# Output projection of the last two token blocks as a seven-product 2x2 block multiplication, and small VectorE instructions given to other engines

## Chip, cores and metric

The kernel runs on one core of a Trainium2 chip. Its time is the device time of one execution in microseconds (us); the figure compared is the median over several runs. One execution of it was also recorded by the hardware profiler. The engines are TensorE (PE in the rows; PEld is its weight load), VectorE (DVE), ScalarE (ACT), GpSimd (POOL) and SyncE (SP), which here issues transfers.

## The reference, cut to what matters

```python
# q, k, v: 4 batches, 8 heads, 576 positions, 64 features
out_d = sm_attn(mean of 4 neighbours of q, k, v)          # 144 x 144 scores per head
out_local = sm_attn(q, k, v, mask=|i - j| < 4)            # a band of 7 keys
x = repeat(out_d, 4) + out_local                          # 2304 tokens x 512
# moe:  w_in 512 x 2048, w_out 2048 x 512, alpha per column
h = x @ w_in
x = (np.maximum(h, 0.0) + alpha * np.minimum(h, 0.0)) @ w_out
# moe2: w_gate, w_val 512 x 1536, w_out 1536 x 512
xn = x / np.sqrt(np.mean(x * x, axis=-1, keepdims=True) + 1e-06) * rms_g
g = xn @ w_gate
return (g * (1.0 / (1.0 + np.exp(-g))) * (xn @ w_val)) @ w_out
```

All of it is in f32.

## The kernel before

**Matmuls.** Each f32 operand is split into an upper half in f16 and a lower half, the f16 of what is left. A product is three f16 matmuls: upper by upper, upper by lower and lower by upper. The helper `split` (L430) makes the halves: ACT writes the upper one (L432), and DVE subtracts it from the scaled source (L433). `halves` (L1646) does the same without a scale, ACT at L1647 and DVE at L1648.

**Blocks and stages.** The 2304 tokens are six blocks of 384 (BW). A block m goes through `m1(m)`, the first expert (products `hps` at L1445, then ReLU parts `g` on ACT and DVE, `ghl` their halves, and the sums over 2048 in four PSUM tiles `acc` at L1462); `m1_evac` takes `acc` to `x1` on ACT (L1476), scaled by a column `inv` that DVE multiplies before it (L1474). Then comes the normalisation: squares on ACT (L1371), their sums `ra` over four pieces on DVE (L1376), a power on POOL (L1397), the factor spread by TensorE into `rps`, and in `xn` the product `ra<-x,rps` (L1419) and its split into the halves `x`. Then `m2(m)`: gate and value products `gps` (L1581), tanh on ACT, the product `th` (L1595) and the value product (L1598) on DVE, the halves `uhl`, and the output product `oacc` (L1610).

**The last two blocks.** Blocks 4 and 5 go through the second expert together in `m2_pair`. Their gate and value products are already a 2x2 block multiplication with seven products (tiles `pa`, `pb`, `pf`, L1758), over 12 groups f of 128 of the 1536 columns. The output product follows (L1819): for each block and each of three tiles of 128 tokens 12 x 3 matmuls of 512 columns, 216 in all. ACT evicts the left half of a tile (L1825) and then DVE the right one (L1826), and a transfer writes it.

**The attention beside it.** The local attention of each block is computed on DVE and POOL, while TensorE does the stages of earlier blocks: POOL multiplies (`prod`, 128x896, L538 with the keys and L592 with the values), and DVE sums (L549, L605). `sm1` and `sm2` are the softmax between them. `trans` transposes the result into the PSUM tile `xps`, DVE adds the downsampled attention into an SBUF tile `xs` (L642), and `split` makes the halves `xt` that `m1` reads.

**Order.** The program is written in groups; the last statement, `issue_order(tc, nc, groups)`, puts the instructions of every engine in a fixed order by a list schedule with costs that stand in the file, and the table `LEADS` shifts ranges of groups by hand (first group, last group, ns). Every engine then works through its own list in that order and waits by semaphores, so an instruction whose operands are late holds up all behind it on its engine.

## Time and profile before

| | |
|---|---|
| median of 3 runs | 948.97 us (948.82 to 949.27) |
| the profiled execution, its own time | 947.25 us |
| its span in the trace | 945.5 us |
| TensorE busy | 911.5 us, 96% of the span |
| VectorE busy | 668.6 us, 71% |
| ScalarE busy | 509.3 us, 54% |
| GpSimd busy | 241.0 us, 25% |

The time of an execution and the span differ by what lies before the first and after the last record. A term that is read from the trace is set against the time of the profiled execution, and that against the median.

The stages by the profile: to 110 us the weights are read and split, and the first dense attention; 110 to 240 the first block's first expert; 240 to 390 the second expert of blocks 0 and 1; 390 to 540 the first expert of blocks 2 and 3; 540 to 610 the second expert of block 2; 610 to 740 the first expert of blocks 4 and 5; 740 to 812 the second expert of block 3; 812 to 894 gate and value of the pair; 894 to 941.2 its output product; then the last eviction and transfer.

### The profile page before, as it was taken

To read this page: it belongs to the slowest core of one execution; us is meant where nothing else is said; L and a number is where in the kernel's file an instruction comes from. 1 tells how busy PE (TensorE), PEld (TensorE's weight loads), DVE (VectorE), ACT (ScalarE), POOL (GpSimd) and SP (SyncE) were. 2 spreads that over 40 slices of the span, in tenths; PEclk is the share of its full clock that TensorE was granted. 3 is DMA by queue.
4 is the path that set the end of the run, shared out by engine and by line. 5 is a ranking of instruction groups with operands and counts; after the bars stand their busy time and mean duration, and the time that the engine had idled before them with its cause. 6 is when DMAs were issued, how large, how long until landed. Compare 5 with 4: busy or idle time off the path is not lost.

```text
span 945.5 us, 16369 instructions
## 1 busy us (share of the span) xinstructions
PE 911.5 (96%) x6412; PEld 589.4 (62%) x6412; DVE 668.6 (71%) x1281; ACT 509.3 (54%) x1163; POOL 241.0 (25%) x167
## 2 busy tenths in 40 slices
PE   6968999999999999999999999999999999999998
PEld 4856878699665565555666555556666565555543
DVE  4789996788899966988876889497476246356510
ACT  5899889789972374233665322243443333456410
POOL 1101100340333405776205668251131000000000
PEclk9989999999999999999999999999999999999999
DMA  9785534446321222221141211010000000100001
GB/s 243 261 263 177 158 118 120 163 140 227 108 84 59 72 86 86 95 79 53 54 124 34 84 51 34 6 29 2 1 1 1 1 1 1 32 3 2 1 23 44
DMA packets 53711, 73.78 MB, mean 78 GB/s; under 512 B 22190, under 2 KB 35138, under 8 KB 53634
## 3 DMA queue, kind: packets, MB, share of 16 engines
q1 hardware_dynamic: 53634, 72.74, 24.9%
q8 instruction: 50, 0.82, 0.3%
q14 instruction: 27, 0.22, 0.1%
...
## 4 chain that ended last, share of the span: by engine, by line
PE 79%; DVE 9%; ACT 8%; DMA 2%; issue 2%; SPq 0%; POOL 0%; ACTq 0%; DVEq 0%; POOLq 0%
PE acc L1462 18%; PE hps L1445 17%; PE gps L1581 16%; PE oacc L1610 7%; PE oacc L1819 5%; PE pa L1758 4%; PE pf L1758 2%; DMA out_dram<-ob 1%; ACT wr L1179 1%; DVE lo L605 1%; PE pb L1758 1%; ACT wi L432 1%; ACT wr L1182 1%; ACT dls L969 1%; PE avps L766 1%
## 5 line engine op out<-in xcount | busy, mean ns | idle before, releaser
L1445 PE MATMUL hps<-xt,wi 128*128 128x192 f16 (+1 forms) x1536 | 324.3, 287 | 6.3 <-DVE g L433 2.3
L1581 PE MATMUL gps<-x,w 128*128 128x384 f16 x1152 | 244.5, 326 | 6.0 <-DVE th L1595 5.2
L1462 PE MATMUL acc<-ghl,wo 128*128 128x384 f16 (+1 forms) x960 | 235.9, 310 | 0.5 <-ACT ob L1639 0.2
L1445 PEld LDWEIGHTS <-wi 128*128 128x128 f16 x1536 | 145.6, 99 | 57.4 <-issue 5.6
L1462 PEld LDWEIGHTS <-wo 128*128 128x128 f16 x1344 | 127.9, 98 | 61.1 <-issue 2.9
L1581 PEld LDWEIGHTS <-w 128*128 128x128 f16 x1152 | 113.0, 99 | 81.0 <-issue 7.9
L1610 PE MATMUL oacc<-w,uhl 128*128 128x512 f16 x432 | 143.5, 379 | 0.0
L538 POOL TENSOR_TENSOR prod<-cq,ckv 128x896 f32<-128x896 f32 x48 | 104.4, 2193 | 130.6 <-ACT dd L735 40.5
L592 POOL TENSOR_TENSOR prod<-ls,ckv 128x896 f32<-128x896 f32 x48 | 86.0, 1867 | 103.2 <-issue 49.7
L1451 DVE SCALAR_TENSOR_TENSOR hps<-g,oma,hps 128x192 f32<-128x192 f32 (+1 forms) x128 | 66.0, 517 | 38.6 <-ACT g L1449 37.4
L1449 ACT ACTIVATE g<-hps 128x384 f32<-128x384 f32 x96 | 47.2, 492 | 82.7 <-PE hps L1445 82.5
L1610 PEld LDWEIGHTS <-uhl 128*128 128x128 f16 x432 | 42.5, 99 | 43.7 <-issue 1.9
L1462 PE MATMUL acc<-g,wo 128*128 128x192 f16 (+1 forms) x384 | 65.8, 286 | 0.0
L432 ACT ACTIVATE ghl<-hps,grp 128x384 f16<-128x384 f32 (+1 forms) x73 | 41.9, 576 | 36.2 <-DVE hps L1451 29.8
L1601 ACT ACTIVATE uhl<-gps 128x384 f16<-128x384 f32 x48 | 23.4, 488 | 58.2 <-DVE gps L1598 43.2
L433 DVE SCALAR_TENSOR_TENSOR ghl<-hps,grp,ghl 128x384 f16<-128x384 f32 (+1 forms) x73 | 44.1, 605 | 14.6 <-ACT ghl L432 14.4
L605 DVE TENSOR_REDUCE lo<-prod 128x128 f32<-128x896 f32 x48 | 51.6, 1078 | 3.6 <-POOL prod L592 3.2
L549 DVE TENSOR_REDUCE ls<-prod 128x14 f32<-128x896 f32 x48 | 51.7, 1077 | 2.4 <-POOL prod L538 2.4
L1719 POOL TENSOR_TENSOR wt<-w 128x768 f32<-128x768 f16 x16 | 26.4, 1650 | 73.4 <-DVE wi L1648 58.8
L1179 ACT ACTIVATE wr<-wr 128x768 f32<-128x768 f32 (+1 forms) x48 | 42.3, 887 | 4.9 <-DMA wr<-in_moe_w_in_dram 2.9
L1819 PE MATMUL oacc<-w,wo 128*128 128x512 f16 x180 | 42.9, 379 | 0.0
L1594 ACT ACTIVATE th<-gps,tsc 128x384 f32<-128x384 f32 x36 | 20.7, 577 | 40.2 <-PE gps L1581 40.2
...
## 6 DMA issues: line engine op xcount, KB each, us to landing
...
```

The source lines that it names most:

```text
L538: engs[i].tensor_tensor(out=pr, in0=view(st["q"][:, j, t:t + TP], [[D, TP], [0, ND], [1, D]]), in1=view(st["k"][:, j, t:t + TP], [[D, TP], ...
L549: nc.vector.tensor_reduce(out=st["s"][:, j, t:t + TP], in_=st.pop(("p", i)), axis=AX.X, op=ALU.add)
L592: engs[i].tensor_tensor(out=over(pr, i), in0=view(st["s"][:, j, t:t + TP], [[ND, TP], [1, ND], [0, D]]), in1=view(st["v"][:, j, t:t + TP], ...
L605: nc.vector.tensor_reduce(out=st["o"][:, t:t + TP, j], in_=view(pr, [[ND * D, TP], [ND, D], [1, ND]]), axis=AX.X, op=ALU.add)
L1179: nc.scalar.activation(out=hi.bitcast(F32), in_=hi.bitcast(F32), func=AF.Prelu, scale=2.0 ** -112, alpha=2.0 ** 32)
L1445: nc.tensor.matmul(ps[:, j], wi[:, f + j, a, kk * 128:(kk + 1) * 128], x[:, b_, kk, c0:c0 + n], start=(i == 0), stop=(i == 3 * KK - 1))
L1451: nc.vector.scalar_tensor_tensor(out=ps[:, j], in0=g[:, j], scalar=oma[:, f + j:f + j + 1], in1=ps[:, j], op0=ALU.mult, op1=ALU.add)
L1462: nc.tensor.matmul(acc[e], wo_f(f)[:, a, e * 128:(e + 1) * 128], hl[:, b_], start=(f == f0 and i == 0), stop=(f == f1 and i == 2))
L1581: nc.tensor.matmul(ps, w2_t[i0 + f // 3].rearrange("p a (k c) -> p a k c", k=KK)[:, a, kk, (f % 3) * 128:(f % 3 + 1) * 128], xh[:, b_, kk] ...
L1610: nc.tensor.matmul(acc[tt], t[:, a, tt * 128:(tt + 1) * 128], w[:, b_, f % 3], start=(f in first and i == 0), stop=(f in last and i == 2))
L1758: nc.tensor.matmul(ps, w[:, a, kk, c:c + 128], x[:, b_, kk], start=(start and n == 0), stop=(n == 3 * K2 - 1), skip_group_check=True)
L1819: nc.tensor.matmul(acc, uhl(f)[:, h, a, tt * 128:(tt + 1) * 128], w[:, b_, f % 3], start=(f == 0 and i == 0), stop=(f == NF2 - 1 and i == 2))
```

## The change

**The output product of the pair** becomes a 2x2 block multiplication with seven products. The blocks are: the two token blocks by two halves of the 1536 columns (6 groups g each), and the weight by its row halves and column halves (256 columns each). `outp` makes one product for one tile of 128 tokens: 6 x 3 matmuls of 256 columns; there are 7 x 3 of these, 378 matmuls, into the PSUM tiles `px` and `py`. `usums` makes the sums and differences of the left operand on POOL, two for each of the first six f and three for each of the last six, and their halves; `wsums` does it for the weights (for each g two sums that put the f32 value back together from its halves, and four differences). `scaled` writes halves with a constant factor, ACT the upper and DVE the lower one. `fma` on DVE adds a product to what was evicted before.

**Small instructions** move from DVE: the sums `ra` of the normalisation, the lower halves `x` in `xn`, and the mask, maximum and normalising steps of the local softmax to POOL; `inv`, `dsum` (12 of 16) and a constant's addition to ACT. The sum of the two attentions stays in PSUM, and `split` reads it there.

**The table of shifts** `LEADS` is new, 53 lines for 45; the first line of each stands for it below. Counted on the two programs: TensorE has 378 matmuls where it had 216 in the output product and is otherwise the same; POOL has 284 instructions for 172, ACT 1068 for 1009, DVE 1239 for 1263.

```diff
-    (5553, 5613, 20500), (6925, 6974, 3000), (8480, 8741, -2500), (3702, 3837, 500), (545, 591, -4500),
+    (8269, 8277, -4000), (3290, 3494, -500), (6599, 6626, -500), (7948, 7994, -15500), (5847, 6045, -12500),
...
-            nc.vector.tensor_tensor(out=s, in0=s, in1=m.unsqueeze(3).to_broadcast([128, 2, T, ND]), op=ALU.subtract)
+            nc.gpsimd.tensor_tensor(out=s, in0=s, in1=m.unsqueeze(3).to_broadcast([128, 2, T, ND]), op=ALU.subtract)
...
-            nc.vector.tensor_scalar(out=m, in0=m, scalar1=1e-9, scalar2=None, op0=ALU.add)
+            nc.scalar.activation(out=m, in_=m, func=AF.Copy, bias=1e-9)
             nc.vector.reciprocal(m, m)
-            nc.vector.tensor_tensor(out=s, in0=s, in1=m.unsqueeze(3).to_broadcast([128, 2, T, ND]), op=ALU.mult)
+            nc.gpsimd.tensor_tensor(out=s, in0=s, in1=m.unsqueeze(3).to_broadcast([128, 2, T, ND]), op=ALU.mult)
...
-                xs = att.tile([128, HP, TH * NC], F32, tag="xs", name="xs")
-                ps = ps.rearrange("p t (c r h) -> p t h c r", h=HP, r=2)
-                xv = xs.rearrange("p h (t c r) -> p t h c r", t=TH, r=2)
+                pv = ps.rearrange("p t (c r h) -> p t h c r", h=HP, r=2)
...
+                        pa = pv[:, a - s0:e - s0, :, :, r]
                         nc.vector.tensor_tensor(
-                            out=xv[:, a - s0:e - s0, :, :, r],
-                            in0=ps[:, a - s0:e - s0, :, :, r],
+                            out=pa, in0=pa,
                             in1=od[:, :, :, o].unsqueeze(1).to_broadcast([128, e - a, HP, NC // 2]),
                             op=ALU.add)
...
-                split(x[:, 0, :, c0:c0 + TH * NC], x[:, 1, :, c0:c0 + TH * NC], xs, col(S_X0 + b))
+                split(x[:, 0, :, c0:c0 + TH * NC], x[:, 1, :, c0:c0 + TH * NC],
+                      view(ps, [[1, HP], [HP, TH * NC]]), col(S_X0 + b))
...
-            nc.vector.tensor_scalar(out=sm, in0=sm, scalar1=1e-9, scalar2=4.0, op0=ALU.add, op1=ALU.mult)
+            nc.scalar.activation(out=sm, in_=sm, func=AF.Copy, scale=4.0, bias=4e-9)
...
-                    nc.vector.tensor_tensor(out=st["a"], in0=st["a"], in1=a, op=ALU.add)
+                    nc.gpsimd.tensor_tensor(out=st["a"], in0=st["a"], in1=a, op=ALU.add)
...
-                nc.vector.tensor_tensor(out=x, in0=x1_t[m][:, e], in1=st["r"], op=ALU.mult)
-                split(xh_t[m][:, 0, e], xh_t[m][:, 1, e], x, rgx[:, e:e + 1])
+                nc.vector.scalar_tensor_tensor(out=x, in0=x1_t[m][:, e], scalar=rgx[:, e:e + 1], in1=st["r"],
+                                               op0=ALU.mult, op1=ALU.mult)
+                nc.scalar.activation(out=xh_t[m][:, 0, e], in_=x, func=AF.Copy)
+                nc.gpsimd.tensor_tensor(out=xh_t[m][:, 1, e], in0=x, in1=xh_t[m][:, 0, e], op=ALU.subtract)
...
-            nc.vector.tensor_tensor(out=inv1[:, b:b + 1], in0=col(INV1_0 + b), in1=col(INVW), op=ALU.mult)
+            if b not in inv_done:
+                inv_done.add(b)
+                nc.scalar.activation(out=inv1[:, b:b + 1], in_=col(INV1_0 + b), func=AF.Copy, scale=col(INVW))
...
+        def scaled(o, x, c):
+            nc.scalar.activation(out=o[:, 0], in_=x, func=AF.Copy, scale=c)
+            nc.vector.scalar_tensor_tensor(out=o[:, 1], in0=x, scalar=c, in1=o[:, 0], op0=ALU.mult, op1=ALU.subtract)
+
+        def wsums(g):
+            ra = att.tile([128, DM], F32, tag="da", name="wr1")
+            rb = ob_p.tile([128, DM], F32, tag="ob", name="wr2")
+            for r, f in ((ra, g), (rb, g + F2)):
+                nc.gpsimd.tensor_tensor(out=r, in0=wof(f)[:, 0], in1=wof(f)[:, 1], op=ALU.add)
+            a1, a2, b1, b2 = ra[:, 0:ED], ra[:, ED:DM], rb[:, 0:ED], rb[:, ED:DM]
+            for o, x, y in ((a1, a2, a1), (a2, b2, a2), (b2, b2, a1), (b1, b1, b2)):
+                nc.gpsimd.tensor_tensor(out=o, in0=x, in1=y, op=ALU.subtract)
+            scaled(t13[g], ra, 0.5)
+            scaled(t2(g), b2, 1.0)
+            scaled(wof(g)[:, :, ED:DM], b1, 1.0)
...
+        def usums(f, ga, gb):
+            g = f % F2
+            G = nc.gpsimd
+            x, y = f32(A21[g]), f32(S3F[g])
+            if f < F2:
+                scaled(two(A11[g]), ga, 1.0)
+                G.tensor_tensor(out=y, in0=ga, in1=x, op=ALU.subtract)
+                scaled(two(S3[g]), y, 0.5)
+                return
+            scaled(two(A12[g]), ga, 1.0)
+            scaled(two(A22[g]), gb, 1.0)
+            G.tensor_tensor(out=x, in0=x, in1=gb, op=ALU.add)
+            G.tensor_tensor(out=y, in0=gb, in1=y, op=ALU.subtract)
+            z = prod_p.tile([128, BW], F32, tag="prod", name="s4")
+            G.tensor_tensor(out=z, in0=ga, in1=y, op=ALU.subtract)
+            scaled(two(S1[g]), x, 0.5)
+            scaled(two(S2[g]), y, 0.25)
+            scaled(two(S4[g]), z, 0.25)
...
-            value(f, ga, A, 0)
-            value(f, gb, s3_, 1)
-
-        for h, m in enumerate((ma, mb)):
-            for tt in range(NT):
-                n = h * NT + tt
-                tag = ("a0", "at", "w", "a1", "at", "a2")[n]
-                acc = pool_of(tag).tile([128, DM], F32, tag=tag, name="oacc")
-                for f in range(NF2):
-                    w = w2_t[8 + f // 3].rearrange("p a (f e) -> p a f e", f=3)
-                    for i, (a, b_) in enumerate(((0, 0), (0, 1), (1, 0))):
-                        nc.tensor.matmul(acc, uhl(f)[:, h, a, tt * 128:(tt + 1) * 128], w[:, b_, f % 3],
-                                         start=(f == 0 and i == 0), stop=(f == NF2 - 1 and i == 2))
-                TQ = 128 // NC
-                tag = "prod" if h == 0 else "raw"
-                o = pool_of(tag).tile([128, DM], F32, tag=tag, name="ob")
-                HD = DM // 2
-                nc.scalar.activation(out=o[:, 0:HD], in_=acc[:, 0:HD], func=AF.Copy, scale=col(INV2))
-                nc.vector.tensor_scalar(out=o[:, HD:DM], in0=acc[:, HD:DM], scalar1=col(INV2), scalar2=None,
-                                        op0=ALU.mult)
-                if h:
-                    b, t = divmod(m * 2 * T + tt * TQ, TT)
-                    assert t + TQ <= TT and b > 0
-                    nc.sync.dma_start(out=bass.AP(tensor=out.tensor, offset=out.offset + (b * S + t) * DM,
-                                                  ap=[[TT * DM, NC], [DM, TQ], [1, DM]]), in_=o)
-                else:
-                    rows_out(o, m, tt)
+            value(f, ga, ga, A)
+            value(f, f32(A21[f]) if f < F2 else gb, gb, s3_)
+            if f == F2 // 2:
+                places()
+            usums(f, ga, gb)
+            if F2 // 2 <= f < F2 // 2 + F2:
+                wsums(f - F2 // 2)
...
-        for h, m in enumerate((ma, mb)):
-            for tt in range(NT):
-                n = h * NT + tt
-                tag = ("a0", "at", "w", "a1", "at", "a2")[n]
-                acc = pool_of(tag).tile([128, DM], F32, tag=tag, name="oacc")
-                for f in range(NF2):
-                    w = w2_t[8 + f // 3].rearrange("p a (f e) -> p a f e", f=3)
-                    for i, (a, b_) in enumerate(((0, 0), (0, 1), (1, 0))):
-                        nc.tensor.matmul(acc, uhl(f)[:, h, a, tt * 128:(tt + 1) * 128], w[:, b_, f % 3],
-                                         start=(f == 0 and i == 0), stop=(f == NF2 - 1 and i == 2))
-                TQ = 128 // NC
...
-                nc.scalar.activation(out=o[:, 0:HD], in_=acc[:, 0:HD], func=AF.Copy, scale=col(INV2))
-                nc.vector.tensor_scalar(out=o[:, HD:DM], in0=acc[:, HD:DM], scalar1=col(INV2), scalar2=None,
-                                        op0=ALU.mult)
...
+        def outp(ps, u, w, tt, start):
+            for g in range(F2):
+                for i, (a, b_) in enumerate(((0, 0), (0, 1), (1, 0))):
+                    nc.tensor.matmul(ps, two(u[g])[:, a, tt * 128:(tt + 1) * 128], w(g, b_),
+                                     start=(start and g == 0 and i == 0), stop=(g == F2 - 1 and i == 2),
+                                     skip_group_check=True)
+
+        def fma(o, ps, c, x):
+            nc.vector.scalar_tensor_tensor(out=o, in0=ps, scalar=col(c), in1=x, op0=ALU.mult, op1=ALU.add)
+
+        oa, ob = [xt_p.tile([128, NT, DM], F32, tag="xt", name="ob") for _ in range(2)]
+        X, s1, s2 = [], [], []
+        for tt in range(NT):
+            tag = ("a0", "w", "at")[tt]
+            x = pool_of(tag).tile([128, 2, ED], F32, tag=tag, name="px")
+            X.append(x)
+            outp(x[:, 1], A12, b2(0), tt, True)
+            outp(x[:, 0], A11, b1, tt, True)
+            t = wk.tile([128, ED], F32, tag="mm", name="so")
+            nc.scalar.activation(out=t, in_=x[:, 0], func=AF.Copy, scale=col(INV2))
+            fma(oa[:, tt, 0:ED], x[:, 1], INV2, t)
+            s1.append(t)
+        for tt in range(NT):
+            outp(X[tt][:, 0], A22, lambda g, b_: wof(g)[:, b_, ED:DM], tt, False)
+            t = hl_p.tile([128, ED], F32, tag="hl", name="so")
+            nc.scalar.activation(out=t, in_=X[tt][:, 0], func=AF.Copy, scale=col(INV2))
+            s2.append(t)
+        for tt in range(NT):
+            tag = ("a1", "w", "at")[tt]
+            F_, G_ = pool_of(tag).tile([128, ED], F32, tag=tag, name="py"), X[tt][:, 1]
+            o4, o5 = oa[:, tt], ob[:, tt]
+            outp(F_, S1, s13(0), tt, True)
+            fma(o5[:, ED:DM], F_, INV8, s1[tt])
+            outp(G_, S2, lambda g, b_: t2(g)[:, b_], tt, True)
+            fma(o4[:, ED:DM], G_, INV8, s1[tt])
+            outp(F_, S4, b2(1), tt, False)
+            fma(o4[:, ED:DM], F_, INV8, o4[:, ED:DM])
+            rows_out(o4, ma, tt)
+            outp(G_, S3, s13(1), tt, False)
+            fma(o5[:, 0:ED], G_, INV8, s2[tt])
+            fma(o5[:, ED:DM], G_, INV8, o5[:, ED:DM])
```

**TensorE, the end of the gate and value products.** `pa` and `pf` are gate products, `oacc` (before) and `px` (after) the output product; behind the arrow stands first the operand that streams through TensorE and then the one that is loaded before it; the names are those of buffers, which hold several things in turn. Before:

```order
L1758 LDWEIGHTS w_4015
L1758 MATMUL pa<-xc,w_4015 128x384
L1819 LDWEIGHTS wo
L1819 MATMUL oacc<-w_3111,wo 128x512
L1758 LDWEIGHTS w_4015
L1758 MATMUL pa<-xc,w_4015 128x384
L1819 LDWEIGHTS wo
L1819 MATMUL oacc<-w_3111,wo 128x512
```

After:

```order
L1825 LDWEIGHTS w_4015
L1825 MATMUL pa<-xc,w_4015 128x384
L1908 LDWEIGHTS wi
L1908 MATMUL px<-w_3803,wi 128x256
L1825 LDWEIGHTS w_4015
L1825 MATMUL pa<-xc,w_4015 128x384
L1825 LDWEIGHTS wi
L1825 MATMUL pf<-xc,wi 128x384
```

Output matmuls stand between the last gate matmuls in both; after the change they have 256 columns.

**TensorE, the first `py` matmul,** the first whose two operands are sums made by POOL (`ts` holds those of the weight, `w_3245` here those of the left operand). After:

```order
L1908 LDWEIGHTS wo
L1908 MATMUL px<-w_3458,wo 128x256
L1908 LDWEIGHTS wi
L1908 MATMUL px<-w_3111,wi 128x256
L1908 LDWEIGHTS w_3245
L1908 MATMUL py<-ts,w_3245 128x256
L1908 LDWEIGHTS wi
L1908 MATMUL px<-w_3111,wi 128x256
```

It stands behind 87 `px` matmuls that follow the last gate product; before the change there are `oacc` matmuls here and no operand from POOL.

**GpSimd, the end of its list.** `wt` are sums for the weights of the gate products, `ry` the power of the normalisation; `wr` are sums of the output weight, `wo` and `s` sums of the left operand (`th`). Before:

```order
L1719 TENSOR_TENSOR wt<-w_3592 128x768
L1719 TENSOR_TENSOR wt<-w_4015 128x768
L1719 TENSOR_TENSOR wt<-w_3935 128x768
L1719 TENSOR_TENSOR wt<-w_4015 128x768
L1719 TENSOR_TENSOR wt<-w_3935 128x768
L1397 TENSOR_TENSOR ry<-ry,mhalf 128x3 x2
```

After:

```order
L1810 TENSOR_TENSOR wr_9912<-w_4145 128x512
L1813 TENSOR_TENSOR wr_9911<-wr_9912,wr_9911 128x256
L1856 TENSOR_TENSOR wo<-th,wo 128x384
L1813 TENSOR_TENSOR wr_9912<-wr_9912,wr_9911 128x256
L1858 TENSOR_TENSOR s_9988<-th,wo 128x384
L1856 TENSOR_TENSOR wo<-th,wo 128x384
L1813 TENSOR_TENSOR wr_9912<-wr_9912 128x256
L1858 TENSOR_TENSOR s_10059<-th,wo 128x384
L1856 TENSOR_TENSOR wo<-th,wo 128x384
L1855 TENSOR_TENSOR wo<-wo,th 128x384 x2
L1858 TENSOR_TENSOR s_10130<-th,wo 128x384
L1855 TENSOR_TENSOR wo<-wo,th 128x384
```

Before, POOL's list ended with the normalisation of the last block; after, it ends with the sums that the output product reads.

**VectorE, from block 3's first expert to block 2's second.** Before:

```order
L433 SCALAR_TENSOR_TENSOR ghl<-hps,grp,ghl 128x384
L605 TENSOR_REDUCE lo<-prod 128x2x64 x2
L1474 TENSOR_TENSOR inv_106<-sc 128x1
L605 TENSOR_REDUCE lo<-prod 128x2x64
L1474 TENSOR_TENSOR inv_106<-sc 128x1
L1376 TENSOR_TENSOR ra<-ra 128x384
L1595 SCALAR_TENSOR_TENSOR th<-th,gps 128x384
L642 TENSOR_TENSOR xs<-xps,outd 128x3x4x16
L1598 SCALAR_TENSOR_TENSOR gps<-th,kap,gps 128x384
L1376 TENSOR_TENSOR ra<-ra 128x384
L1602 TENSOR_TENSOR uhl<-gps,uhl 128x384
```

After:

```order
L442 SCALAR_TENSOR_TENSOR ghl<-hps,grp,ghl 128x384
L614 TENSOR_REDUCE lo<-prod 128x2x64
L650 TENSOR_TENSOR xps<-xps,outd 128x3x4x16
L650 TENSOR_TENSOR xps<-xps,outd 128x2x4x16
L650 TENSOR_TENSOR xps<-xps,outd 128x4x16
L614 TENSOR_REDUCE lo<-prod 128x2x64
L442 SCALAR_TENSOR_TENSOR xt<-xps,sc,xt 128x4x96
L558 TENSOR_REDUCE ls<-prod 128x14
L650 TENSOR_TENSOR xps<-xps,outd 128x4x16
L650 TENSOR_TENSOR xps<-xps,outd 128x2x4x16
L1616 SCALAR_TENSOR_TENSOR th<-th,gps 128x384
```

The two `inv` and the `ra` sums between the reductions and `th` are gone from this list; the sums of the attention now write `xps`, and the lower half `xt` reads it.

## Rows read from the trace of the kernel before

**Rows 1.** Page, the span and part 1: busy time, share and instructions of each engine.

```profile
span 945.5 us, 16369 instructions
...
PE 911.5 (96%) x6412; PEld 589.4 (62%) x6412; DVE 668.6 (71%) x1281; ACT 509.3 (54%) x1163; POOL 241.0 (25%) x167
```

**Rows 2.** Busy time by stretch: length, PE, PEld, DVE, ACT, POOL; PEclk, DMA, GB/s.

```profile
0.00:110.00 110.00, 89.07 (x853) 73.30 (x854) 87.47 (x237) 94.08 (x275) 15.79 (x43) 0.97 0.73 220
...
540.00:610.00 70.00, 66.86 (x385) 37.92 (x384) 56.33 (x88) 18.50 (x38) 41.77 (x24) 1.00 0.12 34
...
812.00:894.00 82.00, 81.69 (x497) 48.35 (x496) 44.69 (x76) 44.62 (x80) 0.00 (x0) 1.00 0.04 10
894.00:941.20 47.20, 47.20 (x221) 21.41 (x219) 7.37 (x14) 6.01 (x11) 0.00 (x0) 1.00 0.08 23
941.20:945.50 4.30, 0.03 (x1) 0.00 (x0) 0.68 (x2) 0.47 (x1) 0.00 (x0) 0.99 0.32 122
```

**Rows 3.** TensorE's timeline, 192-column matmuls: start us, duration, engine, line, operation.

```profile
145.41 2.15 PE L1445 MATMUL hps<-xt,wi 128*128 128x192 f16 x24
147.40 0.33 PE L1462 MATMUL acc<-g,wo 128*128 128x384 f16 x1
```

**Rows 4.** TensorE's timeline, 512-column matmuls of the last stage.

```profile
926.17 11.82 PE L1819 MATMUL oacc<-w,wo 128*128 128x512 f16 x54
937.83 0.38 PE L1819 MATMUL oacc<-w,uhl 128*128 128x512 f16 x1
```

**Rows 5.** TensorE's waits, 110 us on: total us, times, longest us.

```profile
PE gps L1581 <- DVE th L1595: 5.2, 6, 1.3
PE hps L1445 <- DVE ghl L433: 1.3, 2, 0.9
PE qkps L713 <- DVE xs L642: 0.5, 1, 0.5
```

**Rows 6.** TensorE's timeline around 543 us, idle time before it in brackets.

```profile
542.88 2.27 PE L1581 MATMUL gps<-x,w 128*128 128x384 f16 x13 [1.33 <-DVE th L1595]
```

**Rows 7.** VectorE's timeline, two long instructions.

```profile
540.13 1.76 DVE L1474 TENSOR_TENSOR inv<-sc 128x1 f32<-128x1 f32 x1 [0.43 <-ACT x L1476]
...
577.24 2.25 DVE L433 SCALAR_TENSOR_TENSOR x<-ra,rgx,x 128x384 f16<-128x384 f32 x1
```

**Rows 8.** GpSimd's timeline, the products beside them.

```profile
539.78 2.09 POOL L538 TENSOR_TENSOR prod<-cq,ckv 128x896 f32<-128x896 f32 x1 [1.09 <-DVE lo L605]
...
576.99 2.08 POOL L538 TENSOR_TENSOR prod<-cq,ckv 128x896 f32<-128x896 f32 x1 [1.24 <-issue]
```

**Rows 9.** VectorE's groups by form: count, busy us, mean ns, idle before.

```profile
L433 DVE SCALAR_TENSOR_TENSOR ghl<-hps,grp,ghl 128x384 f16<-128x384 f32 x71 | 43.3, 611 | 14.5 <-ACT ghl L432 14.4
...
L433 DVE SCALAR_TENSOR_TENSOR xt<-xs,sc,xt 128x384 f16<-128x384 f32 x16 | 17.7, 1109 | 0.1
L1648 DVE TENSOR_TENSOR wo<-th,wo 128x384 f16<-128x384 f32 x20 | 15.6, 786 | 7.3 <-ACT wo L1647 6.9
L433 DVE SCALAR_TENSOR_TENSOR x<-ra,rgx,x 128x384 f16<-128x384 f32 x16 | 14.9, 944 | 0.0
...
L1376 DVE TENSOR_TENSOR ra<-ra 128x384 f32<-128x384 f32 x15 | 8.5, 564 | 2.7 <-ACT ra L1371 2.7
L1474 DVE TENSOR_TENSOR inv<-sc 128x1 f32<-128x1 f32 x9 | 8.4, 939 | 5.8 <-ACT x L1476 5.8
```

**Rows 10.** GpSimd's groups by form.

```profile
L1719 POOL TENSOR_TENSOR wt<-w 128x768 f32<-128x768 f16 x16 | 26.4, 1650 | 73.4 <-DVE wi L1648 58.8 <-DVE wsr L1648 10.3 <-DVE wt L1724 4.0
L979 POOL TENSOR_TENSOR dls<-dls,dlsum 96x408 f32<-96x408 f32 x12 | 11.2, 955 | 106.7 <-DVE eb L425 60.6 <-DVE sc L1261 25.8 <-ACT g L1449 9.2
...
L1397 POOL TENSOR_TENSOR ry<-ry,mhalf 128x3 f32<-128x3 f32 x6 | 5.2, 873 | 76.5 <-DVE ry L1396 75.5 <-DVE eb L425 0.9
```

**Rows 11.** ScalarE's timeline, the last eviction.

```profile
941.27 0.47 ACT L1825 ACTIVATE ob<-oacc,sc 128x256 f32<-128x256 f32 x1 [0.39 <-PE oacc L1819]
```

**Rows 12.** VectorE's timeline, the last eviction.

```profile
941.77 0.48 DVE L1826 TENSOR_SCALAR ob<-oacc,sc 128x256 f32<-128x256 f32 x1 [0.38 <-ACT ob L1825]
```

More of the change, by code (lines that the diff above doesn't have):

```diff
@@ L398 @@
     INV1_0 = S_X0 + B
+    INV8 = INV1_0 + B
     def eb(i):
@@ L1466, in m1_acc @@
         return [ps_a.tile([128, n], F32, tag=f"a{e}", name=f"acc{e}") for e in range(KK)]
+    inv_done = set()
     def m1_evac(m, acc, c0, n):
@@ L1739, in m2_pair @@
             scr += [w2_t[4 + i][:, a, 0:PW].bitcast(F32) for a in range(2)]
-        last = {}
-        def uhl(f):
-            if f < 10:
-                t = wo[:, f * 2 * BW:(f + 1) * 2 * BW]
-            else:
-                if not last:
-                    last["t"] = raw_p.tile([128, 4 * BW], F32, tag="raw", name="uhl")
-                t = last["t"][:, (f - 10) * 2 * BW:(f - 9) * 2 * BW]
-            return t.bitcast(F16).rearrange("p (h a n) -> p h a n", h=2, a=2)
+        F2, ED = NF2 // 2, DM // 2
@@ new lines, in m2_pair, with part @@
+        wif = wi.rearrange("p f a c -> p (f a c)")
+        w2f = {i: w2_t[i].rearrange("p a w -> p (a w)") for i in range(3)}
+        def part(t, n):
+            return t[:, n * 2 * BW:(n + 1) * 2 * BW]
+        wos = [wo[:, n * BW:(n + 1) * BW].bitcast(F16) for n in range(21)]
+        spare = []
+        freed = [[part(w2f[1], n) for n in range(4)] + [part(wif, n) for n in range(8)] +
+                 [w2_t[4 + i][:, a, PW:2 * PW] for i in (0, 1) for a in range(2)],
+                 [part(w2f[2], n) for n in range(4)] + [part(wif, 8 + n) for n in range(8)] +
+                 [w2_t[6][:, a, PW:2 * PW] for a in range(2)]]
@@ new lines, in m2_pair, with places @@
+        A11, A21, S3F, S3 = wos[0:F2], wos[F2:2 * F2], wos[2 * F2:3 * F2], wos[3 * F2:]
+        A12, A22, S1, S2, S4 = [], [], [], [], []
+        t13, t4 = [], []
+        def places():
+            r = raw_p.tile([128, 4 * BW], F32, tag="raw", name="us").bitcast(F16)
+            S3.extend(part(r, n) for n in range(3))
+            freed[1].append(part(r, 3))
+            for l in freed:
+                for g in range(3):
+                    for x, n in zip((A12, A22, S1, S2, S4), range(5)):
+                        x.append(l[5 * g + n])
+            for _ in range(2):
+                t = raw_p.tile([128, 4 * BW], F32, tag="raw", name="ts").bitcast(F16)
+                t13.extend(t[:, g * 2 * DM:(g + 1) * 2 * DM].rearrange("p (a e) -> p a e", a=2) for g in range(3))
@@ new lines, in two, with f32, wof, t2 @@
+        def two(x):
+            return x.rearrange("p (a n) -> p a n", a=2)
+        def f32(x):
+            return x.bitcast(F32)
+        def wof(f):
+            return w2_t[8 + f // 3].rearrange("p a (f e) -> p a f e", f=3)[:, :, f % 3]
+        def t2(g):
+            return w2f[0][:, g * DM:(g + 1) * DM].rearrange("p (a e) -> p a e", a=2)
+        def scaled(o, x, c):
+            nc.scalar.activation(out=o[:, 0], in_=x, func=AF.Copy, scale=c)
+            nc.vector.scalar_tensor_tensor(out=o[:, 1], in0=x, scalar=c, in1=o[:, 0], op0=ALU.mult, op1=ALU.subtract)
@@ L1771, in gate, with value @@
             return th
[L1773 to L1774 removed]
+        def value(f, o, u, v):
+            nc.vector.scalar_tensor_tensor(out=o, in0=u, scalar=kps[:, f // 3:f // 3 + 1], in1=v, op0=ALU.mult,
                                            op1=ALU.mult)
[L1776 to L1781 removed]
+        def usums(f, ga, gb):
[16 more added lines that the diff above has]
+            scaled(two(S4[g]), z, 0.25)
         xa, xb = xh_t[ma], xh_t[mb]
@@ new lines, in m2_pair @@
+        for tt in range(NT):
[17 more added lines that the diff above has]
+            fma(o5[:, ED:DM], G_, INV8, o5[:, ED:DM])
+            TQ = 128 // NC
+            b, t = divmod(mb * 2 * T + tt * TQ, TT)
+            assert t + TQ <= TT and b > 0
+            nc.sync.dma_start(out=bass.AP(tensor=out.tensor, offset=out.offset + (b * S + t) * DM,
+                                          ap=[[TT * DM, NC], [DM, TQ], [1, DM]]), in_=o5)
```

36 lines of the change are left out of this document (20 added, 16 removed), and 96 rows, old and new, of the table LEADS.

## Prediction

> **What bounds the kernel now.** I read the page's busy shares first. TensorE is busy for 911.5 of 945.5 us, and no other engine comes near [rows 1]. The table of stretches shows where the other 34 us are: 20.9 us in the first 110 us, while the weights are split, and 4.3 us behind the last matmul [rows 2]. Between 110 and 941.2 us TensorE is busy for 911.48 - 89.07 - 0.03 = 822.4 of 831.2 us and idle for 8.8 us. So in those 831 us only two things shorten the kernel: less work in TensorE's stream, or fewer of these 8.8 us. A faster DVE, ACT or POOL is worth nothing by itself.
>
> For the stream I took the pitch of back-to-back matmuls, the distance between starts, not the duration that a row prints, which overlaps with the next. 24 matmuls of 192 columns take 147.40 - 145.41 = 1.99 us, 0.083 us each [rows 3]; 54 of 512 columns take 937.83 - 926.17 = 11.66 us, 0.216 us each [rows 4]. Both have a new 128x128 weight load for every matmul.
>
> For the 8.8 us I took TensorE's waits: six waits of the gate matmuls for the DVE product th are 5.2 us, the largest 1.3; two for the lower half of ghl are 1.3; one for xs is 0.5 [rows 5]. What is late there? At 542.88 TensorE has waited 1.33 us for th [rows 6]. In front of th on DVE stands a product of one column, inv, which took 1.76 us [rows 7], though it has 128 elements in all. A POOL product had started 0.35 us before it and ran for 2.09 us [rows 8]; DVE ended with it. The same is seen at 577.24: the lower half x took 2.25 us [rows 7], beside a POOL product from 576.99 that took 2.08 [rows 8]. On average such a half with two SBUF operands takes 0.94 to 1.11 us, and the same half with its source in PSUM 0.61 [rows 9].
>
> The Trainium skill (SBUF — State Buffer, "SBUF: two separate sides") says that a DVE instruction with two SBUF inputs and a GpSimd instruction that reads SBUF share one port pair, and that whichever starts first holds it for the whole instruction. The trace agrees: the two pairs just named end 0.02 and 0.42 us after each other.
>
> **The change part by part.**
>
> *The output projection of the last two blocks.* It removes 216 matmuls of 512 columns and adds 378 of 256. Removed: 216 x 0.2159 = 46.6 us; the stage as a whole is 47.2 us, all busy [rows 2]. The trace has no 256-column matmul with 128 weight columns in f16. Between the rows for 192 and 512, the straight line gives 0.083 + (64/320) x 0.133 = 0.1095 us: 378 x 0.1095 = 41.4 us, **-5.3 us**. The bounds: strictly proportional to 512 columns 0.108 (-5.8); if a 256-column matmul had 10% more overhead, 0.119 (-1.7). I take the line, since 192 columns already show no visible floor.
>
> The Trainium skill (TensorE: Matmul & The Clock Gate, "Back-to-back issue gap") gives for a stream of weight load and matmul 81 ns at 128 columns and 131 ns at 512. Halfway by columns, about 98 ns at 256 as an estimate, 216 x 0.131 = 28.3 us would become 378 x 0.098 = 37.0, 8.7 us slower. The 54 matmuls of rows 4 speak against that figure for 512 columns; the measurement decides.
>
> *What the new product needs beside it.* POOL, which did nothing after 812 us [rows 2], gets 24 sums of 128x384, 12 of 512 and 24 of 256. By its f32 rows [rows 10], 955 ns for 408 columns and 1650 for 768, a sum of 384 is 0.93 us, of 512 1.15, of 256 0.62: 22.3 + 13.8 + 14.9 = 51 us. They may begin when the first of 12 groups f is through, about 823 us (82/12 = 6.8 us per f, and its chain), and the first matmul of the product that needs the sums (py) stands behind the last gate product and some 87 px matmuls (87 x 0.1095 = 9.5 us), at about 903. So 80 us hold 51. DVE loses 24 lower halves, 6 evictions, and gains 60 halves and 18 combinations: 42 of 384 at 0.61 and 18 smaller ones, 35 us, less 24 x 0.79 = 19 [rows 9], plus 18 - 6 instructions at 0.48 [rows 12]: +22 us on some 52 of the 129 us [rows 2]. ACT by the same count gains about 14 on some 51 [rows 2]. Both have room: cost **0**, if each piece comes in time. The last f's chain is what can be late: value 0.6, five POOL sums 4.7, upper half 0.5, lower half 0.6, with the gate before it 1.2 and hand-offs: about 8.6 us, against 9.5 us of px and 16 py matmuls (1.8) before its operand is used. It fits by 2 to 3 us; a small wait or two of TensorE on DVE is likely: **+0.8** (0 to 3). Without the cover the whole 8.6 would show.
>
> *The end.* Before, ACT and DVE evict the last tile one after the other, 0.47 + 0.48 us [rows 11, 12], then the transfer. After, two DVE combinations of the same size run one after the other: **+0.3** (-0.3 to 0.6).
>
> *Small work off DVE.* Nine inv products (0.94 on average) become three on ACT, 15 ra sums (0.56) and 16 lower halves x go to POOL, 16 lower halves xt read PSUM, since xs is no longer written to SBUF (as in the row of ghl, 0.61 for 1.11) [rows 9]; the mask, maximum and sum steps of the local attention go to POOL and ACT. On DVE that is 8 + 8 + 15 + 8 us and, with the small ones and xs kept in PSUM at the same price, some 45 of its 668.6 us [rows 1]. By itself that is worth nothing; through the waits it is worth what stood behind these instructions. Going through the waits of rows 5 one by one: of the six for th one of 1.0 us lies behind a weight split that stays; the other five (4.15 us) lie behind inv, x, xt or a dsum that was held up; add the wait for xs (0.5) and the smaller one for ghl (0.4). That is 5.1 us. The POOL products remain and DVE instructions with two SBUF operands remain too, so some of these waits come back elsewhere: I take three quarters, **-3.8** (0 to -5.1).
>
> POOL gets 31 instructions of 384 columns there, 29 us, and some 20 small ones. It is busy for 41.8 of 70 us in its fullest stretch [rows 2]. A sum may queue behind one product of 2.1 us [rows 8]: the ra sums lead to the normalisation, a pow on POOL itself (0.87) and only then to the x that the next gate matmuls read. This costs nothing as long as the other block's matmuls cover it; without them it is 2.1 us per queueing, which is in the rival below.
>
> The Trainium skill (GPSIMD Engine Reference, "Engine selection") puts elementwise sums on VectorE and calls GpSimd about 2x slower for two inputs, which speaks against these moves. By rows 9 and 10 the lower half x has nothing to lose: 0.94 on DVE against about 0.93.
>
> *The head.* The table of shifts is new, and the first 110 us have their own order. ACT's work there is 94.1 of 110 us [rows 2], and in the new order its last weight split stands two instructions later, the first ReLU five earlier: **0** (-2 to +2).
>
> Sum: -5.3 + 0.8 + 0.3 - 3.8 + 0 = **-8.0**. The profiled execution took 947.25 us for a span of 945.5; it lies 1.7 us below the median of 948.97. Against the median: **941.0 us**; the two times of before differ by less than the terms do, so I expect the profiled execution at about 939.
>
> **The rivals.**
>
> *Only the stream gets shorter.* The waits for th go, and new ones come for x, which now stands in POOL's queue behind products of 2.1 us. For it: x goes through three engines now (DVE, ACT, POOL). Against it: a lower half held up by POOL did take 2.2 us too. Time: 948.97 - 5.3 + 1 = 944 to 945. Chance 0.20.
>
> *More is gained.* All 5.1 us come back, no new wait, and the head is 1 to 2 us shorter: 937.5 to 939.5. Chance 0.10.
>
> *Head or hand-offs cost.* The new order costs 3 us in the first 110 us, or the last f comes 4 us late: 945.5 to 948.5. Chance 0.09.
>
> *Slower: POOL and DVE take turns in the last 120 us.* Each of the 60 new DVE halves reads two SBUF operands, and if none of them can overlap with a POOL sum, as at 540 and 577 us, then 51 + 35 = 86 us stand in 80: py starts 6 us late, 947 us. It decides from there: if a sum of 384 takes 1.0 us or more instead of 0.93 (51 x 1.08 + 35 - 80 = 10), the kernel is slower than before, and at 1.2 us it is 66 + 35 - 80 = 21 us late, 962. For it: rows 7 and 8 show that taking of turns. Against it: the sums are short, DVE is idle for half of this stage, and by the f32 row of 408 columns 0.93 is well founded. Chance 0.06.
>
> *The small matmuls don't run at the line's pitch,* so that 378 cost as much as 216 or more (0.123 us each and above): 946 to 950. The 192-column row, 0.083, speaks against it. Chance 0.02.
>
> **How the numbers follow.** The forecast has chance 0.53, its own range 939.5 to 943.5. Two runs of this kernel that differ by under 0.2%, 1.9 us, can't be told apart. Faster (below 947.07): forecast, stream only, more gained, and half of the last three; 0.53 + 0.20 + 0.10 + 0.04 = 0.87, which I lower to 0.86. Within 0.2%: 0.08. Slower (over 950.87): 0.06. The range from 937.5 to 946.5 holds the first three cases and the cheaper half of the fourth.
>
> **What would show it.** Right: some 378 matmuls of 256 columns at a pitch near 0.109; TensorE's idle time from 110 us to the last matmul at 5 to 6 us; no inv, x or dsum of over 1.5 us on DVE; POOL's last sum before about 903 us. Wrong: a wait of py for DVE of several us (the POOL rival), waits of gps for x on POOL (stream only), a first 110 us with more than 23 us of idle TensorE, or a pitch of 0.12.

## The result, and the profile after

The changed kernel takes **938.09 us** (median of 4 runs, 936.82 to 939.32), the kernel before 948.89 in the same comparison: a ratio of 0.9881 (95% interval 0.9863 to 0.9899), 10.8 us less. The forecast was 941.0 in a range of 937.5 to 946.5. The profiled execution took 936.82 us with a span of 935.1.

The page of the changed kernel, span and part 1:

```profile
span 935.1 us, 16829 instructions
...
PE 909.3 (97%) x6574; PEld 608.4 (65%) x6574; DVE 662.0 (71%) x1257; ACT 520.4 (56%) x1222; POOL 337.7 (36%) x279
```

Against [rows 1] TensorE has 162 more matmuls and is idle for 25.8 us of the span instead of 34.0; GpSimd works 97 us more. Where it went is seen best by counting matmuls up to fixed times. Busy time by stretch, columns as in [rows 2], of the kernel before, in three stretches in which both kernels do the same work but for the moved instructions:

```profile
0.00:240.00 240.00, 218.91 (x2214) 183.61 (x2215) 195.27 (x486) 210.32 (x526) 36.54 (x55) 0.99 0.61 187
240.00:610.00 370.00, 362.31 (x2277) 216.60 (x2275) 302.99 (x531) 168.12 (x400) 172.45 (x93) 1.00 0.22 69
610.00:812.00 202.00, 201.33 (x1212) 119.43 (x1211) 117.59 (x174) 79.78 (x147) 32.01 (x20) 1.00 0.02 5
```

and of the changed kernel:

```profile
0.00:240.00 240.00, 222.44 (x2194) 185.20 (x2195) 191.75 (x472) 210.96 (x534) 41.55 (x62) 0.99 0.61 188
240.00:610.00 370.00, 368.92 (x2329) 221.54 (x2328) 273.34 (x479) 171.43 (x418) 197.78 (x134) 1.00 0.22 69
610.00:812.00 202.00, 201.54 (x1218) 119.83 (x1217) 111.05 (x169) 79.37 (x147) 38.74 (x26) 1.00 0.02 5
```

After 240 us the changed kernel is 20 matmuls behind (20 x 222.44/2194 = 2.0 us). From 240 to 610 it does 52 more in the same time, 52 x 362.31/2277 = 8.3 us, and TensorE's idle time there falls from 7.69 to 1.08 us; from 610 to 812 it gains 6 more, 1.0 us. The count takes matmuls of all widths as equal; weighed with the pitch of each width in the two traces, the stretches give +2.1, -8.0 and -0.4 us, so the split is good to about 1 us. The waits for th, 5.2 us in [rows 5], are gone. All waits of TensorE from 110 us on that the trace lists:

```profile
PE hps L1462 <- DVE ghl L442: 1.2, 2, 0.8
PE ssps L1392 <- POOL ra L1385: 0.7, 1, 0.7
PE acc L1479 <- DVE x L1565: 0.4, 1, 0.4
PE acc L1479 <- ACT ob L1660: 0.4, 1, 0.4
PE pa L1825 <- ACT ob L1660: 0.3, 1, 0.3
PE allps L417 <- ACT w L1201: 0.2, 1, 0.2
```

TensorE's idle time from 110 us to its last matmul is 818.68 - 815.40 = 3.3 us, for 8.8 before:

```profile
110.00:928.68 818.68, 815.40 (x5731) 532.19 (x5728) 575.57 (x1021) 426.91 (x951) 321.61 (x236) 1.00 0.19 60
```

None of the waits is of `px` or `py`. The last stage, by stretch, and the end:

```profile
812.00:890.00 78.00, 77.72 (x487) 47.45 (x486) 60.96 (x97) 50.30 (x106) 49.02 (x49) 1.00 0.03 8
890.00:926.00 36.00, 36.00 (x332) 32.26 (x330) 22.30 (x36) 8.34 (x20) 10.56 (x10) 1.00 0.04 11
```

The last pieces of the chain that ended last:

```profile
923.77 4.93 PE px L1908 x45
928.72 0.48 DVE ob L1913
```

Forty-five matmuls of 256 columns in 4.93 us are 0.1096 us each; 0.1095 was forecast. TensorE ends at 928.7 us, 12.5 us earlier than before (941.2, [rows 2]), but the span ends 6.4 us behind it instead of 4.3. VectorE and GpSimd by form:

```profile
L442 DVE SCALAR_TENSOR_TENSOR xt<-xps,sc,xt 128x384 f16<-128x384 f32 x16 | 9.8, 610 | 0.8 <-ACT xt L441 0.7
```

```profile
L1437 POOL TENSOR_TENSOR x<-ra,x 128x384 f16<-128x384 f32 x16 | 16.4, 1029 | 21.9 <-ACT x L1436 21.5
L1385 POOL TENSOR_TENSOR ra<-ra 128x384 f32<-128x384 f32 x15 | 15.7, 1044 | 24.3 <-ACT ra L1380 24.3
...
L1855 POOL TENSOR_TENSOR wo<-wo,th 128x384 f32<-128x384 f32 x6 | 7.4, 1236 | 0.0
L1856 POOL TENSOR_TENSOR wo<-th,wo 128x384 f32<-128x384 f32 x6 | 7.2, 1200 | 3.4 <-DVE th L1841 3.4
L1858 POOL TENSOR_TENSOR s<-th,wo 128x384 f32<-128x384 f32 x6 | 6.8, 1126 | 1.4 <-DVE wi L1804 1.4
```

The half xt with its source in PSUM takes 610 ns for the 1109 of [rows 9]. A GpSimd sum of 384 columns was put at 0.93 us and takes 1.03 to 1.24.

### The profile page after: what moved, and what is told of

It is laid out like the page before. It is cut to its first block, busy times and chain, and to the rows that moved or that the text cites. A ratio compares the mean times of both kernels' runs of the same rounds, so it can differ in the third digit from the quotient of the medians.

```text
span 935.1 us, 16829 instructions
## 1 busy us (share of the span) xinstructions
PE 909.3 (97%) x6574; PEld 608.4 (65%) x6574; DVE 662.0 (71%) x1257; ACT 520.4 (56%) x1222; POOL 337.7 (36%) x279
## 4 chain that ended last, share of the span: by engine, by line
PE 86%; DMA 4%; ACT 4%; DVE 3%; issue 1%; SPq 0%; POOL 0%; DVEq 0%; ACTq 0%
PE gps L1602 20%; PE acc L1479 18%; PE hps L1462 18%; PE oacc L1631 9%; PE pa L1825 4%; PE px L1908 3%; DMA out_dram<-ob 2%; PE pf L1825 2%; PE py L1908 1%; PE pb L1825 1%; DMA wr<-in_moe_w_in_dram 1%; PE sps L734 1%; PE avps L774 1%; PE lsps L957 1%; DMA wr<-in_moe_w_gate_dram 1%
## 5 line engine op out<-in xcount | busy, mean ns | idle before, releaser
L1462 PE MATMUL hps<-xt,wi 128*128 128x192 f16 (+1 forms) x1536 | 342.0, 289 | 4.1 <-DVE ghl L442 1.2
L1479 PE MATMUL acc<-ghl,wo 128*128 128x384 f16 (+1 forms) x960 | 245.1, 310 | 0.9 <-DVE x L1565 0.4
L1602 PE MATMUL gps<-x,w 128*128 128x384 f16 x1152 | 238.1, 326 | 0.0
L1462 PEld LDWEIGHTS <-wi 128*128 128x128 f16 x1536 | 148.4, 100 | 59.7 <-issue 6.7
L1631 PE MATMUL oacc<-w,uhl 128*128 128x512 f16 x432 | 139.7, 379 | 0.0
L547 POOL TENSOR_TENSOR prod<-cq,ckv 128x896 f32<-128x896 f32 x48 | 100.4, 2111 | 74.7 <-PE avps L774 50.8
L1479 PE MATMUL acc<-g,wo 128*128 128x384 f16 (+1 forms) x384 | 68.8, 286 | 0.0
L987 POOL TENSOR_TENSOR dls<-dls,dlsum 96x408 f32<-96x408 f32 x12 | 11.8, 1005 | 110.2 <-ACT g L441 61.4
```

Source lines behind the costliest of these rows:

```text
L547: engs[i].tensor_tensor(out=pr, in0=view(st["q"][:, j, t:t + TP], [[D, TP], [0, ND], [1, D]]), in1=view(st["k"][:, j, t:t + TP], [[D, TP], ...
L1462: nc.tensor.matmul(ps[:, j], wi[:, f + j, a, kk * 128:(kk + 1) * 128], x[:, b_, kk, c0:c0 + n], start=(i == 0), stop=(i == 3 * KK - 1))
L1479: nc.tensor.matmul(acc[e], wo_f(f)[:, a, e * 128:(e + 1) * 128], hl[:, b_], start=(f == f0 and i == 0), stop=(f == f1 and i == 2))
L1602: nc.tensor.matmul(ps, w2_t[i0 + f // 3].rearrange("p a (k c) -> p a k c", k=KK)[:, a, kk, (f % 3) * 128:(f % 3 + 1) * 128], xh[:, b_, kk] ...
L1631: nc.tensor.matmul(acc[tt], t[:, a, tt * 128:(tt + 1) * 128], w[:, b_, f % 3], start=(f in first and i == 0), stop=(f in last and i == 2))
```

## Experiments

**Without the shifts: four kernels.** To part the change from its new table, `LEADS` was emptied in the kernel before, in it with the moves off VectorE alone, in it with the seven products alone, and in the changed kernel.

```diff
-LEADS = (
...
+LEADS = ()
```

The kernel before: 

> The kernel before with an empty table of shifts. If the table is worth much, 958 to 975 us; if the list schedule alone is as good, 949. It is the base for the next three, whose order comes from the same rules without any shift by hand.

The moves alone: 

> No shifts, output projection as before, only the small work moved off VectorE. Theory A (these moves give what lies beyond the shorter stream): 5 to 9 us under the run without shifts of the kernel before. Theory B (the new shifts give it, the moves little): within 2 us of it. Theory C (work in GpSimd's queue holds TensorE up): 2 us or more over it.

The seven products alone: 

> No shifts, only the seven-product output projection, the small work stays on VectorE. Stream alone: 5.4 us less work for TensorE, 2.1 us more behind the last matmul, so 3 to 4 us under the run without shifts of the kernel before. If the new sums on GpSimd hold up the last stage where nobody tuned it: 0 to 4 us over it.

Both: 

> The changed kernel with an empty table of shifts. Theory A: the sum of the two single parts, 8 to 12 us under the run without shifts of the kernel before. Theory B: 3 to 5 us under it, and the rest of the 10.8 us between the two tuned kernels is the tables'.

| no shifts | median us | ratio to the kernel before (95%) |
|---|---|---|
| kernel before | 949.46 | 0.9998 (0.9985 to 1.001) |
| moves alone | 943.25 | 0.9927 (0.991 to 0.9943) |
| seven products alone | 944.63 | 0.9945 (0.9928 to 0.9963) |
| both | 941.69 | 0.9909 (0.9894 to 0.9923) |

The old table was worth nothing that can be measured. By the medians the moves give 6.2 us by themselves, within theory A's 5 to 9. The products give 4.8, more than the 3 to 4 of the stream alone. Together they give 7.8, not 11.0, which lies between the ranges of the two theories (8 to 12 and 3 to 5): on top of the products the moves give only 2.9 (944.63 to 941.69). From 240 to 610 us, without shifts, in this order: kernel before, moves alone,

```profile
240.00:610.00 370.00, 366.00 (x2312) 219.70 (x2311) 295.93 (x543) 171.75 (x405) 173.75 (x93) 1.00 0.22 71
```

```profile
240.00:610.00 370.00, 370.00 (x2352) 223.25 (x2350) 273.10 (x481) 174.14 (x423) 202.89 (x134) 1.00 0.23 70
```

and both:

```profile
240.00:610.00 370.00, 367.33 (x2317) 220.14 (x2317) 273.82 (x480) 171.94 (x419) 193.29 (x133) 1.00 0.22 70
```

With the moves alone TensorE has no idle time left there, 4.00 us less, and does 40 matmuls more. But up to 240 us it had done 28 fewer (2153 for 2181), and the two profiled executions are only 3.4 us apart (947.09 and 943.72; the first was the fastest of ten). So the traces show that the moves remove stalls, and not the whole 6.2 us of the medians. With both, 2.67 us are idle again. The list schedule gives each of these kernels an order of its own, and no run parts what comes from the moved work and what from the order. Of the 10.8 us the new table holds about 3 (941.69 to 938.09 is 3.6 by the medians, 2.7 by the two ratios). The two intervals touch (0.9894 and 0.9899), so this is rough.

**Single moves under the old shifts.** All moves, only inv, and only the lower halves x, each in the kernel before with its table. The edit of the second:

```diff
-            nc.vector.tensor_tensor(out=inv1[:, b:b + 1], in0=col(INV1_0 + b), in1=col(INVW), op=ALU.mult)
+            nc.scalar.activation(out=inv1[:, b:b + 1], in_=col(INV1_0 + b), func=AF.Copy, scale=col(INVW))
```

> The kernel before with its own shifts and all the moves off VectorE (inv as nine on ScalarE, so that the shifts still meet the same instructions). Theory A: 942 to 945 us, the waits behind inv, x and xt gone and TensorE idle for 3 to 5 us from 110 us to its last matmul instead of 8.8. Theory B: 947 to 951, since shifts made for another program are worth nothing.

> The kernel before with its shifts, only the nine inv products on ScalarE. If the wait of 1.33 us at 543 us and the one of 0.40 at 539 come from inv beside a GpSimd product: both gone, 1 to 2 us faster, 947 to 948. If DVE was late there anyway: a wait of over 1 us stays near 543 us, 949.

> The kernel before with its shifts, only the 16 lower halves x on GpSimd. If the x halves of over 2 us on DVE cause the waits between 577 and 591 us (1.8 us in the trace): these gone, 947 to 948. If a place in GpSimd's queue costs as much: gate matmuls wait for GpSimd's x instead, 949 or more.

They took 969.98, 961.99 and 962.93 us (ratios 1.0225, 1.0136 and 1.0148), slower by 12 to 20 us. All three expectations failed. With nine tiny instructions moved, the waits from 110 us on are at new places:

```profile
PE acc L1462 <- ACT ghl L432: 2.8, 4, 1.1
PE hps L1445 <- DVE ghl L433: 2.7, 4, 1.2
PE acc L1462 <- DVE ghl L433: 1.4, 2, 1.2
```

The shifts still name the same instructions, but the schedule that they are added to is another. This shows far from the moved work: with inv alone moved, TensorE's order differs from that of the kernel before from 10.6 us on, though the first inv runs at 155 us, and up to 240 us it does 2094 matmuls for 2214. All the moves together gained 6.2 us with no table and lost 20 with the old one, so it is the old table that spoils the new schedule. What one single move is worth can't be had in this way, and stays open.

**The last stage: which engine makes the sums.** `nc.gpsimd` became `nc.vector` in `usums` and `wsums`.

```diff
-            G = nc.gpsimd
+            G = nc.vector
...
```

> The changed kernel with the 60 sums of the last stage on VectorE instead of GpSimd. VectorE is busy for some 61 of 78 us from 812 to 890 in the changed kernel, and the sums are 24 x 0.56 + 36 x about 0.45 = 30 us more, less what it waits for GpSimd now. If VectorE has no room: py late by 4 to 10 us, 942 to 948. If the taking of turns with GpSimd costs as much as it saves: 937 to 939.

It took 938.13 us (0.9857, 0.9841 to 0.9874). VectorE is busy for 66.0 of the 78 us from 812, not 90, and TensorE for 36.00 of 36 from 890:

```profile
812.00:890.00 78.00, 77.59 (x483) 47.01 (x481) 66.01 (x139) 48.84 (x103) 0.00 (x0) 1.00 0.03 8
890.00:926.00 36.00, 36.00 (x325) 31.59 (x324) 23.04 (x50) 11.47 (x24) 0.00 (x0) 1.00 0.04 9
```

VectorE's busy time over both stretches rises only from 83.3 to 89.1 us, though it has 56 instructions more there: its own had been long because GpSimd's stood beside them. Two of its groups from 812 us on in the changed kernel, the first with an operand in PSUM (`pf`), the second with both in SBUF:

```profile
L1833 DVE TENSOR_TENSOR w<-pf,w 128x384 f32<-128x384 f32 x18 | 10.0, 553 | 2.0 <-PE pf L1825 1.7
...
L1804 DVE SCALAR_TENSOR_TENSOR wi<-th,wi 128x384 f16<-128x384 f32 x8 | 7.8, 984 | 0.1
```

and with GpSimd idle:

```profile
L1833 DVE TENSOR_TENSOR w<-pf,w 128x384 f32<-128x384 f32 x18 | 9.9, 553 | 3.7 <-ACT w L1830 3.2 <-PE pf L1825 0.4
...
L1804 DVE SCALAR_TENSOR_TENSOR wi<-th,wi 128x384 f16<-128x384 f32 x8 | 4.2, 550 | 0.0
```

The half with both operands in SBUF falls from 984 to 550 ns, the instruction that reads PSUM stays at 553. The two ways cost the same within the noise (the intervals of the ratios, 0.9857 and 0.9881, overlap), and part of any difference is the list schedule's, whose order differs from 406 us on. My bound of 4 to 10 us was wrong.

**More work for GpSimd.** A second sum in front of each of the 24 sums of the left operand, into a tile that is written again before anyone reads it:

```diff
+            def again():
+                k = len(nc.cur_bb.bb.instructions)
+                G.tensor_tensor(out=z, in0=ga, in1=gb, op=ALU.add)
...
```

> The changed kernel with a second GpSimd sum of 128x384 in front of each of the 24 sums of the left operand, into a scratch tile that nobody reads: 24 x 1.15 = 28 us more on GpSimd. By the forecast's room (80 us for 60 that it now works): py up to 8 us late, 938 to 946. If DVE and GpSimd took turns strictly, 60 + 28 + 35 = 123 us in 80: 40 us late, 978.

It took 954.68 us (1.0044, 1.0029 to 1.0058), 16.6 us more than the changed kernel (15.5 by the two ratios).

```profile
890.00:926.00 36.00, 27.36 (x189) 19.75 (x187) 33.70 (x36) 13.42 (x28) 31.84 (x28) 0.82 0.00 0
```

GpSimd and VectorE are busy almost throughout, TensorE waits for 8.6 us in this stretch, and its granted clock is 0.82 there. So the slower rival's cliff is there, but 28 us of GpSimd work away and not at 0.07 us per sum; and it is neither the 8 us of free room nor the 40 of strict turns.

**The end, first try: three tiles one after the other.**

```diff
+    for names, by in early:
+        for n in names:
+            lead[at[n]] = by - 6000.0
...
```

> The changed kernel; only the priorities of the last 12 products are changed so that the three token tiles end one after the other. If the longer tail (6.4 us behind the last matmul for 4.3) comes from three transfers of 256 KB issued within 2.4 us: tail about 4.5, 935 to 937 us. If it comes from something else, or the new order makes TensorE wait: 938 or more.

It took 938.60 us (0.9886, 0.9854 to 0.9917). Its tiles do end one by one: SyncE's last two issues are 1.9 us apart, at 930.54 and 932.46 us. Yet the last matmul ends at 931.5 and the span at 938.0, again 6.5 us. So it is not enough to space the last transfers out.

**Second try: how a transfer is cut.** Block 4's tiles lie time-major, so one transfer has 4 x 32 rows; block 5's has 32 x 4. The packets that begin in half a microsecond, counted in the trace of the changed kernel:

```
from 925.5 to 928.5 us (block 4's tiles alone until 927.2):  8 19 20 19 25 28
from 928.5 to 932.0 us (block 5's tiles too):               68 61 40 84 68 92 57
from 932.0 to 934.0 us (what is left):                      27 17 13 7
kernel before, last tile, from 942.5 us:                    66 82 96 44
```

Alone, the 4 x 32 form moves some 20 to 28 packets in 0.5 us; 32 x 4 moves 66 to 96. The last ones of the changed kernel trickle out behind it.

```diff
-            step = min(TQ - done, TT - t)
+            step = min(TQ - done, TT - t, most)
...
-            rows_out(o4, ma, tt)
+            rows_out(o4, ma, tt, 1)
```

> The changed kernel; only the transfer of block 4's tiles is cut into one of 32 rows for each of four time steps, instead of one with 4 x 32 rows. If the longer tail comes from these transfers, which in the trace move about 24 packets of 2 KB in 0.5 us where those of block 5 move 66 to 96: the last landing comes 4.3 to 5 us behind the last matmul instead of 6.4, 936 to 937 us. If the number of late transfers is what counts, or SyncE's extra issues: 938 or more.

It took 938.98 us (0.988, 0.9858 to 0.9902), and yet the tail is cured: the last matmul ends at 936.8, the span at 941.2, 4.4 us. The list schedule made a new order, with waits in the last stage that the changed kernel does not have and that are as long as the gain:

```profile
PE px L1908 <- DVE ob L1913: 1.2, 1, 1.2
PE py L1908 <- DVE ob L1913: 0.9, 1, 0.9
```

This profiled execution took 942.97 us, the longest of the four (the others 938.25 to 939.04). Up to 240 us it does 2134 matmuls for the 2194 of the changed kernel, though the order there is the same, so that its late end is not the edit's.

**Third try: the same transfers, the old order.** The four pieces are priced in the schedule as one transfer. In the two traces the order of TensorE, VectorE, ScalarE and GpSimd is then the same, instruction by instruction.

```diff
+    for k in count:
+        if insts[k].name in priced:
+            dur[k], held[k] = priced[insts[k].name]
...
```

> The changed kernel with block 4's last transfers cut as in the run with the rows apart, but priced in the list schedule as one transfer, so that TensorE, VectorE, ScalarE and GpSimd have exactly the order of the changed kernel. If the cut transfers shorten the tail and the new order ate that in the run before: no wait of py or px in the last stage, the end 4.3 to 4.8 us behind the last matmul, 1.5 to 2 us under the changed kernel, a ratio of 0.986 to 0.987. If the tail's gain is lost to SyncE's twelve issues: 0.988.

It took **935.06 us** (median of 5, 934.77 to 936.31; ratio 0.985, 0.9829 to 0.9871), the lowest median here. Its last matmuls on TensorE's timeline, and its span:

```profile
929.11 1.26 PE L1920 MATMUL px<-ts,us 128*128 128x256 f16 x10
```

```profile
span 934.6 us, 16837 instructions
```

929.11 + 1.26 = 930.37, so the span ends 4.2 us behind the last matmul, 2.2 us less than in the changed kernel, though three transfers of block 5 are still issued within 3 us at the end. The medians differ by 3.0 us; what goes beyond 2.2 lies within the spread of the runs (2.5 us for the changed kernel), and the two intervals (0.9871 and 0.9863) overlap a little, so it is the trace that shows the tail.

## Why the prediction came out as it did

The side and the range were right. Two terms of the sum were mis-sized in opposite directions, so that the time came as near as it did in part by luck.

- **The stream, -5.3.** Right. 0.1096 us for 0.1095, 378 x 0.1096 = 41.4 for 46.6: -5.2. The products alone, without shifts, gave 4.8 with the longer tail in it.
- **The stalls, -3.8 (0 to -5.1).** This step failed: it measured -8.3 from 240 to 610 us and -1.0 to 812, against +2.0 before 240, so **-7.3** (-6.3 with the matmuls weighed by width), outside its bounds either way. I took only waits that I could put down to an instruction, and gave back a quarter. In fact idle time in 240 to 610 fell by 6.6 us, small waits too; from 110 us on 3.3 us are left, where I looked for 5 to 6. And idle time undercounts a stall, because the profile's matmul bars, whose ends are modelled, overlap. One gate matmul of the kernel before on TensorE's timeline:

```profile
540.84 0.33 PE L1581 MATMUL gps<-x,w 128*128 128x384 f16 x1
```

  It shows 0.33 us, but the 13 in [rows 6] begin (2.27 - 0.33)/12 = 0.162 us apart. A stall shows only what goes beyond 0.17 us, so the 8.8 us of idle time were no upper bound. The moves alone, without shifts, show that the moves do remove stalls: no idle time is left in this stretch. How much of the -7.3 is theirs and how much the new table's stays open, since without shifts they gave 6.2 us alone and 2.9 on top of the products.
- **Hand-offs in the last stage, +0.8.** They cost 0: no wait of px or py. GpSimd is busy for 49.02 + 10.56 = 59.6 us there instead of 51, and its last sum ends at 902.5 us, before 903, as I expected. The straight line of [rows 10] gives 0.91 and 0.66 us for 384 and 256 columns, where I wrote 0.93 and 0.62; the sum, 51.6, is nearly the same.
- **The tail, +0.3 (-0.3 to 0.6).** This step failed too: **+2.1**. I compared the two evictions, which are equal, and took the transfer behind them as given. Before, the last packet of block 4's slow transfers began before 932.5 us of 945.5; seven products finish both blocks together. The rows cut apart show it: with them the span ends 4.4 and 4.2 us behind the last matmul.
- **The head, 0.** +2.0 us at 240 (counted in the -7.3), at the edge of the bounds. One execution's head says little: five of the later runs have the changed kernel's order up to 240 us on all four engines and are 9 to 60 matmuls behind it there.
- **Rivals.** The time lies in the range of "more is gained" (937.5 to 939.5, chance 0.10), below the forecast's own 939.5 to 943.5. But that case wanted a head 1 to 2 us shorter, and the head was 2.0 longer. Half of the last three chances is 0.085 and not 0.04, so my sum for "faster" should have been 0.92. Only the stream shorter: wrong, no gate matmul waits for GpSimd's x. POOL and DVE in turns: they do take turns in places. At 895.40 us two halves on DVE took 2.38 us beside two sums on GpSimd at 896.05 that took 2.59:

```profile
895.40 2.38 DVE L1804 SCALAR_TENSOR_TENSOR wi<-th,wi 128x384 f16<-128x384 f32 x2
```

```profile
896.05 2.59 POOL L1855 TENSOR_TENSOR wo<-wo,th 128x384 f32<-128x384 f32 x2
```

  With GpSimd idle such a half took 0.55 us for 0.98, so VectorE did pay for it. But the sums took 1.0 us and more, the point from which I had this rival decide, and nothing was late; the doubled sums put that point far beyond. I had added all 35 us of halves to GpSimd's time, as if each met a sum.

Sum of what was measured, before and after: -5.2 - 7.3 + 0 + 2.1 = -10.4, the difference of the spans. That it meets it to the digit is chance, as the stalls are known to about 1 us.
